# New hand-written engine orders behind the second score fill of a memory-augmented attention with a gated MLP

## The chip, the cores and the metric

The kernel runs on one core of a Trainium2 chip. A core has five engines that take their own instruction queues in order: PE (TensorE, matrix multiply), ACT (ScalarE), DVE (VectorE), POOL (GpSimd) and SP (SyncE, which here only issues DMAs). The metric is the device time of one execution in microseconds (us), the median of several runs.

## The reference

One sequence of 2048 tokens of width 512 goes through two branches, and a gate mixes them.

```python
q, k, v = x @ wq, x @ wk, x @ wv            # 32 heads of 16, 4 segments of 512 tokens
for s in range(4):
    p = softmax(qs @ ks.T * 0.25 + causal_mask)
    a_dot = p @ vs
    a_mem = (phi(qs) @ M) / (phi(qs) @ z + 1e-6)
    o = sigmoid(beta) * a_mem + (1 - sigmoid(beta)) * a_dot
    M = M + phi(ks).T @ vs;  z = z + phi(ks).sum()
a = concat(o) @ wo                          # phi(t) = t + 1 if t > 0 else exp(t)
b = (gelu(x @ w_gate) * (x @ w_up)) @ w_down    # inner width 1792
out = g * a + (1 - g) * b                   # g = sigmoid((x * gate_w).sum(-1))
```

All inputs and the output are bfloat16.

## The kernel before

The work is cut into some 1,200 named tasks, and `ORDER` is a table with one list of names for each engine: that is the order in which the engine executes. A name carries the segment first: `G0_12.2` is segment 0, tile 12 of the gate product, the piece that begins with its third matmul.

On PE, a *whole* task writes one PSUM bank of 128 x 512 and is cut into pieces of two matmuls (line 531): K, Q and V are the projections (four tiles each and segment), G and U the 14 tiles of the gate and up products, D the 4 token tiles of the down product with the wo product (18 matmuls: for segments 0 to 2 the four wo ones first, for segment 3 last). `qk0_1A1` is a *fill*: the scores of segment 0, head group 1, part A1, written as four row tiles into the four banks X (line 906). Parts A0, B0, A1, B1 are the two key halves of the even and the odd heads; part L, once in two head groups, is the diagonal's low corner. `numx1` is the memory's numerator and is filled in the same way (line 826). `pv0_1_0` is a P*V *burst* of 32 small matmuls in column tiles of 32 (lines 954 and 962), `mz0` a memory update (line 873), in column tiles as well. `num1` is a single matmul of the memory.

Whether a K, Q, V, G, U, D or num matmul runs whole or as four column tiles of 32 isn't written in the list: `column_runs` looks at each run of tasks between two fills, and if a burst or memory update stands in it, all matmuls of the run are issued as column tiles (line 533), so that PE keeps one mode in the run.

```python
for c in range(0, P, 32):
    r = e.matmul(view()[c:c + 32, :], lhsT[:, c:c + 32], rhs, start=first, stop=last,
                 tile_position=(0, c))
```

Beside the four X banks there are four banks W, which all whole tasks, bursts and updates share. A bank is free again when its contents are copied out: `K0_3ev`, `Vev0_1`, `Gev0_12` (lines 551 on ACT and 554 on DVE), `Um0_4` (gelu result times the up product, line 1053), `pvt0_0_1` (transposition of a burst's result, line 968), `mzacc0`, `fin`. Each such task stands in the list of ACT or of DVE.

After a fill, ACT makes `exp` of all four X banks (line 912), and the next fill may begin only then. POOL sets the causal corner of the result to zero (`msk`, line 915); a burst needs the masks of its parts and of L. DVE ends a head group with `norm` (lines 980 to 986), which needs both transposed bursts and `GdT`, the gates. The gates come from `gexp` (ACT, line 673), `gmat` (DVE, lines 676 to 679), `gbd` (POOL, lines 681 and 687: nine operations) and `omg` (POOL), and from the sums `gmul` and `gsum` over x times gate_w, `gexs` (ACT) and `exsT` (POOL, line 813). `mzbd0` on DVE (lines 887 and 892) multiplies the new memory by gbd; `numx1` and `num1` need it. `numd1`, `nump1` and `numl1` divide (lines 838 to 855) and free X and num1's bank. `pke`, `pkc`, `pqe`, `pqc` are the phi functions on ACT and DVE, `kp` (lines 763, 772) and `kl` (751) the padded keys.

SP issues the DMAs: `x2_0` to `x2_3` are transposing loads of segment 2's x (line 564; they wait for exp0_1B1), `w_wu`, `w_wd`, `w_wo` weights (each waits for an exp), `pkT` and `oTd` transpositions, `xt1` the untransposed x for gmul1 (it waits for mz0), `Vlo` copies of V rows for the low corner, `out` the results.

`schedule` walks the five lists with estimated durations. It doesn't change their order; its modelled times decide which of the four W banks a group takes, from the constants SWITCH (a change of mode), HOP (from one engine to another) and others.

Of the kernel before, what the change touches and what calls it, by code (L numbers as in the profile page):

```python
# [1203 lines left out]
```

## Time and profile before

| what | value |
|---|---|
| median of 3 runs | 264.63 us (264.21 to 264.8) |
| the profiled execution: time | 265.65 us |
| its span, first to last instruction | 264.4 us |
| granted TensorE clock, mean | 1.00 |
| PE matmuls at line 533 (column tiles) | 1348 instructions |

The profile's page gives busy times and shares, the chain of work that ended last, and groups of instructions; the timeline lists instructions in order of time (start us, length us, engine, line, operation, output<-inputs, shape, count, and in brackets the idle time before them with what ended it). A matmul's end in the timeline is modelled, so lengths overlap by some 0.16 us: the distance between two starts is what counts. PE is the matmul, PEld its weight load. "x10" counts instructions; one matmul in column tiles is four of them.

### The profile page before, as it was taken

What the parts mean: (1) busy time and instruction counts of PE and PEld (TensorE: products, weight loads), DVE (VectorE), ACT (ScalarE), POOL (GpSimd) and SP (SyncE); (2) the same over time, 40 slices, a digit from 0 to 9 for tenths busy, and PEclk for the clock granted to TensorE, in tenths of its full rate; (3) what the DMA queues carried; (4) which work ended last, traced back from release to release, by engine and by line L of the source; (5) the groups of instructions that cost most, each with busy time, mean ns of one, the idle gap of its engine ahead of it and who ended that gap; (6) DMA issues with size and microseconds to landing.
All of it is one profiled execution on the core that took longest, in us unless ns stands there. A gap on an engine that the chain in (4) does not pass through costs nothing.

```text
span 264.4 us, 9416 instructions
## 1 busy us (share of the span) xinstructions
PE 259.4 (98%) x4164; PEld 120.0 (45%) x4164; DVE 196.6 (74%) x369; ACT 212.2 (80%) x190; POOL 106.0 (40%) x256
## 2 busy tenths in 40 slices
PE   8799999999999999999999999999999999999996
PEld 4444445344544444544444444543455434454454
DVE  1589998898998978767795877679895765637363
ACT  3589999889999798799968888789986786877822
POOL 8216843815003464461460164256460233316520
PEclk9999999999999999999999999999999999999999
DMA  6973033940006956120003413310002031000102
GB/s 217 282 198 62 4 72 101 331 141 2 5 6 166 170 84 61 44 82 0 2 2 85 71 32 62 103 41 1 4 2 42 2 84 44 12 30 2 42 2 82
DMA packets 32776, 18.37 MB, mean 69 GB/s; under 512 B 20576, under 2 KB 32736, under 8 KB 32736
## 3 DMA queue, kind: packets, MB, share of 16 engines
q1 hardware_dynamic: 31632, 16.73, 27.5%
q10 hardware_dynamic: 1104, 1.05, 1.2%
q8 instruction: 32, 0.52, 0.8%
q14 instruction: 8, 0.07, 0.1%
HBM read 9.84 MB, written 2.10 MB: 45 GB/s over the span
## 4 chain that ended last, share of the span: by engine, by line
PE 91%; DMA 3%; DVE 2%; POOL 2%; ACT 1%; issue 1%; ACTq 0%; DVEq 0%
PE psW L531 47%; PE psW L533 25%; PE psXALL L906 9%; PE psW L954 5%; DMA wk<-in_A_wk_dram 3%; PE psXALL L533 1%; PE psW L962 1%; PE psXALL L531 1%; POOL gbd L681 1%; ACT pt L912 1%; PE psXALL L826 1%; DVE mzbd L892 1%; PE psW L873 0%; POOL pt L915 0%; DVE obf L984 0%
## 5 line engine op out<-in xcount | busy, mean ns | idle before, releaser
L912 ACT ACTIVATE pt<-psXALL 128x2048 bf16<-128x2048 f32 x64 | 120.1, 1876 | 23.2 <-PE psXALL L906 19.8
L915 POOL TENSOR_SCALAR_AFFINE_SELECT pt<-pt 128x256 bf16<-128x256 bf16 x128 | 57.3, 457 | 119.9 <-ACT pt L912 114.9
L1053 DVE TENSOR_TENSOR hT<-psW,hT 128x512 bf16<-128x512 f32 x56 | 37.6, 686 | 19.0 <-PE psW L531 15.0
L968 DVE STREAM_TRANSPOSE tb<-psW 128x512 f32<-128x512 f32 x32 | 22.3, 707 | 19.5 <-PE psW L962 19.3
L531 PE MATMUL psW<-wd,hT 128*128 128x512 bf16 x136 | 35.5, 380 | 0.0
L531 PE MATMUL psW<-xT,wu 128*128 128x512 bf16 x132 | 34.9, 380 | 0.0
L531 PE MATMUL psW<-xT,wg 128*128 128x512 bf16 x138 | 34.0, 379 | 0.0
L915 POOL TENSOR_SCALAR_AFFINE_SELECT ptl<-ptl 128x512 bf16<-128x512 bf16 x32 | 23.2, 726 | 10.9 <-ACT ptl L912 9.3
L906 PE MATMUL psXALL<-qT,kpad 32*128 32x320 bf16 (+3 forms) x512 | 25.4, 273 | 0.0
L533 PE MATMUL psW<-xT,wu 128*32 128x512 bf16 x368 | 22.0, 379 | 0.0
L533 PE MATMUL psW<-xT,wg 128*32 128x512 bf16 x344 | 20.9, 379 | 0.0
L1037 ACT ACTIVATE hT<-psW 128x512 bf16<-128x512 f32 x28 | 15.3, 598 | 6.6 <-PE psW L533 3.5
L813 POOL COPY exsT<-exs 32x4 f32<-32x4 f32 x64 | 14.1, 220 | 15.9 <-ACT exs L804 12.2
L531 PEld LDWEIGHTS psW<-xT,wg 128*128 128x128 bf16 x138 | 12.9, 98 | 16.0 <-DVE hT L554 0.5
L531 PEld LDWEIGHTS psW<-wd,hT 128*128 128x128 bf16 x136 | 12.5, 98 | 15.8 <-issue 2.1
L533 PE MATMUL psW<-wd,hT 128*32 128x512 bf16 x296 | 19.4, 380 | 0.0
L954 PE MATMUL psW<-pt,vaug 128*17 128x192 bf16 (+3 forms) x512 | 19.3, 273 | 0.0
L531 PE MATMUL psW<-xT,wk 128*128 128x512 bf16 (+1 forms) x74 | 17.2, 334 | 2.0 <-DMA wk<-in_A_wk_dram 1.5
L906 PEld LDWEIGHTS psXALL<-qT,kpad 32*128 32x128 bf16 x512 | 7.6, 92 | 24.7 <-ACT pt L912 14.0
L912 ACT ACTIVATE ptl<-psXALL 128x2048 bf16<-128x2048 f32 x8 | 15.0, 1878 | 4.6 <-PE psXALL L906 4.6
L531 PEld LDWEIGHTS psW<-xT,wu 128*128 128x128 bf16 x132 | 11.7, 98 | 14.7 <-issue 1.9
L531 PE MATMUL psW<-wv,xT 128*128 128x512 bf16 x58 | 16.5, 380 | 0.0
(122 smaller groups left out, 372.3 us busy)
## 6 DMA issues: line engine op xcount, KB each, us to landing
out_dram<-ost SPq DMA_DIRECT2D x15, 128.0 KB, 1.8
wg<-in_B_w_gate_dram SPq DMA_DIRECT2D x2, 896.0 KB, 7.9
wu<-in_B_w_up_dram SPq DMA_DIRECT2D x2, 896.0 KB, 7.0
wd<-in_B_w_down_dram SPq DMA_DIRECT2D x2, 896.0 KB, 5.7
phkt<-in_A_x_dram SPq DMA_DIRECT2D x3, 512.0 KB, 3.8
vlow<-vaug SPq DMA_DIRECT2D x8, 136.0 KB, 2.7
hT<-in_A_x_dram SPq DMA_DIRECT2D x2, 256.0 KB, 3.9
wq<-in_A_wq_dram SPq DMA_DIRECT2D x2, 256.0 KB, 6.1
```

The costliest lines, as they stand in the source:

```text
L531: return e.matmul(view(), lhsT, rhs, start=first, stop=last)
L533: r = e.matmul(view()[c:c + 32, :], lhsT[:, c:c + 32], rhs, start=first, stop=last, tile_position=(0, c))
L681: gb = task("gbd", POOL, [Instr(lambda e, c=c, j=j: e.tensor_tensor(gbd[32 * c:32 * c + 32, :, j, 0:16], gmat[32 * c:32 * c + 32, 2 * c + ...
L813: cross = task(f"exsT{s}", POOL, [Instr(lambda e, g=g, c=c: e.tensor_copy(exsT[sl][32 * g:32 * g + 32, c:16:4], exs[32 * c:32 * c + 32, s4 ...
L826: task(f"numx{s}", PE, [Instr(lambda e, g=g, i=i, qt=qt, t=t: e.matmul(X[g][:, 34 * i:34 * i + 34], phq[32 * g:32 * g + 32, t, qt * 128:(q ...
L906: instrs.append(Instr(lambda e, g=g, lhs=lhs, rhs=rhs, c0=c0, ncol=ncol: e.matmul(X[g][:, c0:c0 + ncol], lhs(32 * g), rhs(32 * g), start=T ...
L912: exp_task(s, f"exp{s}_{t}{name}", [Instr(lambda e: e.activation(dst[:], XALL[:, :].rearrange("p (g c) -> p g c", g=4), ACTF.Exp, scale=AT ...
L915: task(f"msk{s}_{t}{name}", POOL, [Instr(lambda e, view=view, pat=pat, base=base: e.affine_select(out=view, in_=view, compare_op=ALU.is_ge ...
L954: instrs.append(Instr(lambda e, t=t, q=q, kb=kb, slot=slot, c0=c0: e.matmul(gp.f32()[32 * q:32 * q + 17, 128 * kb + 64:512], Vaug[sl][:, k ...
L968: task(f"pvt{s}_{t}_{j}", DVE, [Instr(lambda e: e.transpose(Tb[:, j, :], gp.f32()[:, :]), [gp.key], [("Tb", j)], dve_t(512))], grp=gp)
L1037: lambda e, g=g, ft=ft, s=s: e.activation(hT[s % 2][:, ft, :], g.f32()[:, :], ACTF.Gelu_apprx_tanh),
L1053: task(f"Um{s}_{ft}", DVE, [Instr(lambda e, g=g, ft=ft: e.tensor_tensor(hT[sl][:, ft, :], g.f32()[:, :], hT[sl][:, ft, :], ALU.mult), [g.k ...
```

## The change

All five lists are made anew behind the second fill (`qk0_0B0`); up to there they are the same, apart from the places of DVE, ACT and POOL tasks that lie beside it. The same tasks are executed, with the same operations. 22 tasks of copying, summing and scaling go from ACT to DVE and 20 from DVE to ACT. Of the matmuls that can be tiled, 236 stand in a run with a burst or update in place of 337. In the planner, SWITCH and HOP get other values, and the change of mode is counted before a task's start instead of behind its end. The diff, cut to the first 65 us of PE and what goes with them, and PE's and SP's ends:

```diff
-SWITCH = 0.097
+SWITCH = 0.1
...
-        "V0_2.2 K0_2.4 K0_2.5 K0_2.6 K0_2.7 qk0_0A0 V0_0.0 G0_2.0 V0_0.2 G0_2.2 K0_3.4 V0_1.0 qk0_0B0 V0_3.0 "
-        "V0_3.2 K0_3.5 V0_1.2 K0_3.6 Q1_3.0 qk0_0L Q1_0.0 Q1_3.2 Q1_0.2 G0_1.0 K0_3.7 qk0_0A1 G0_1.2 Q1_1.0 "
-        "G0_12.0 Q1_1.2 G0_12.2 qk0_0B1 G1_10.0 G1_5.0 G1_5.2 G1_10.2 G1_9.0 qk0_1A0 pv0_0_0 G1_7.0 G1_7.2 G1_9.2 "
-        "G0_3.0 qk0_1B0 K1_0.0 G0_3.2 G0_6.0 K1_0.2 G0_6.2 qk0_1A1 pv0_0_1 G0_5.0 G0_5.2 G0_7.0 Q1_2.0 qk0_1B1 "
-        "Q1_2.2 G0_10.0 V1_1.0 V1_1.2 G0_7.2 qk0_2A0 G0_10.2 G1_11.0 G1_11.2 G1_2.0 G1_2.2 qk0_2B0 pv0_1_0 mz0 "
-        "pv0_1_1 G1_1.0 qk0_2L G1_8.0 G1_12.0 G1_12.2 G1_1.2 G1_8.2 qk0_2A1 V1_0.0 V1_0.2 K1_1.0 G1_6.0 G1_6.2 "
-        "qk0_2B1 K1_1.2 G0_9.0 G0_9.2 V1_3.0 K1_2.0 qk0_3A0 K1_2.2 V1_3.2 G1_0.0 G1_0.2 K1_3.0 K1_3.2 qk0_3B0 "
-        "pv0_2_0 G0_4.0 Q2_1.0 G0_4.2 Q2_1.2 G0_13.0 qk0_3A1 pv0_2_1 Q2_0.0 G0_13.2 Q2_0.2 G0_0.0 qk0_3B1 Q2_3.0 "
-        "G0_11.0 G0_0.2 G1_3.0 G1_3.2 Q2_3.2 G0_11.2 G0_8.0 num1 numx1 G1_4.0 G1_4.2 U0_4.0 G0_8.2 U0_4.2 U0_0.0 "
-        "U0_0.2 U0_1.0 U0_1.2 U0_3.0 U0_6.0 U0_3.2 G1_13.0 U0_9.0 U0_6.2 G1_13.2 U0_9.2 U0_5.0 U0_7.0 U0_5.2 "
-        "U0_11.0 U0_8.0 U0_7.2 U0_2.0 U0_2.2 U0_8.2 U1_5.0 U0_11.2 pv0_3_1 U1_5.2 qk1_0A0 pv0_3_0 U0_10.0 U0_10.2 "
-        "U1_0.0 U1_0.2 U1_8.0 U1_6.0 U1_6.2 U0_13.0 U0_13.2 qk1_0B0 U1_2.0 U1_12.0 U1_1.0 U1_12.2 U1_2.2 U1_8.2 "
...
-        "D3_1.8 D3_0.8 D3_2.12 D3_0.10 D3_1.10 D3_2.14 D3_1.12 pv3_3_1 D3_0.12 D3_3w0.0 D3_3w1.0 D3_3w0.4 D3_0.14 "
-        "D3_1.14 D3_3w0.8 D3_3w0.12 D3_1.16 D3_0.16 D3_2.16 D3_3a0.0 D3_3w1.4 D3_3w1.8 D3_3w1.12 D3_3a1.0 "
+        "V0_2.2 K0_2.4 K0_2.5 K0_2.6 K0_2.7 qk0_0A0 V0_0.0 G0_2.0 V0_0.2 G0_2.2 K0_3.4 V0_1.0 qk0_0B0 K0_3.5 "
+        "V0_1.2 V0_3.0 K0_3.6 K0_3.7 Q1_0.0 V0_3.2 qk0_0L Q1_0.2 G0_1.0 Q1_3.0 G0_1.2 Q1_3.2 qk0_0A1 G0_12.0 "
+        "G0_12.2 G0_3.0 G0_3.2 G1_10.0 qk0_0B1 G1_9.0 G1_7.0 G1_10.2 G1_9.2 G1_7.2 qk0_1A0 G1_5.0 Q1_2.0 G0_7.0 "
+        "G1_5.2 G0_7.2 pv0_0_0 qk0_1B0 K1_0.0 K1_0.2 V1_1.0 Q1_1.0 Q1_1.2 qk0_1A1 Q1_2.2 V1_1.2 G0_5.0 G1_12.0 "
+        "G0_5.2 qk0_1B1 pv0_0_1 G0_10.0 G1_12.2 G0_10.2 G1_2.0 G1_2.2 qk0_2A0 G1_1.0 G1_1.2 G0_6.0 G1_11.0 G0_6.2 "
+        "G1_11.2 qk0_2B0 mz0 pv0_1_0 V1_3.0 pv0_1_1 qk0_2L V1_3.2 G1_6.0 V1_0.0 V1_0.2 K1_3.0 qk0_2A1 K1_2.0 "
+        "K1_3.2 G1_6.2 K1_2.2 G1_0.0 qk0_2B1 Q2_1.0 G0_8.0 G1_8.0 G1_0.2 Q2_1.2 G0_8.2 qk0_3A0 G1_8.2 K1_1.0 "
+        "G0_4.0 K1_1.2 G0_4.2 pv0_2_1 qk0_3B0 G1_4.0 G1_4.2 G0_0.0 G0_0.2 pv0_2_0 qk0_3A1 Q2_0.0 G0_13.0 G0_9.0 "
+        "Q2_0.2 G0_9.2 qk0_3B1 num1 G0_13.2 G1_3.0 G1_3.2 Q2_3.0 Q2_3.2 numx1 G0_11.0 G0_11.2 U0_0.0 G1_13.0 "
+        "G1_13.2 U0_0.2 U0_1.0 U0_1.2 U0_2.0 U0_6.0 U0_2.2 U0_5.0 U0_5.2 U0_8.0 U0_3.0 U0_6.2 U0_3.2 U0_11.0 "
+        "U0_11.2 U0_8.2 U0_13.0 U0_13.2 U1_6.0 U1_6.2 U0_9.0 U1_0.0 U0_9.2 U1_0.2 U0_7.0 U0_7.2 U0_4.0 U1_5.0 "
+        "U1_5.2 qk1_0A0 U0_4.2 U1_9.0 U1_8.0 U1_8.2 U1_9.2 U1_1.0 U1_12.0 U1_12.2 U0_12.0 pv0_3_0 qk1_0B0 U1_1.2 "
+        "U1_7.0 U1_7.2 U0_12.2 pv0_3_1 qk1_0L U1_2.0 V1_2.0 V1_2.2 U1_3.0 U1_2.2 qk1_0A1 U1_3.2 D0_2.0 V2_3.0 "
...
+        "qk3_3B1 D3_2.6 D3_2.8 D3_0.10 pv3_3_0 D3_1.12 D3_3w0.0 D3_2.10 pv3_3_1 D3_2.12 D3_0.12 D3_3w0.4 D3_0.14 "
+        "D3_1.14 D3_3w0.8 D3_3w0.12 D3_2.14 D3_2.16 D3_1.16 D3_3w1.0 D3_0.16 D3_3a0.0 D3_3w1.4 D3_3w1.8 D3_3w1.12 "
+        "D3_3a1.0 "
...
-        "Vev0_2 exp0_0A0 Vev0_0 exp0_0B0 gsum0_1 exp0_0L K0_3ev exp0_0A1 gexs0 gexp exp0_0B1 pke0_1 exp0_1A0 "
-        "Gev1_7 exp0_1B0 K1_0ev exp0_1A1 pqe1_0 exp0_1B1 Q1_2ev exp0_2A0 Gev0_10 exp0_2B0 pqe1_1 exp0_2L Gev1_12 "
-        "exp0_2A1 Vev1_0 exp0_2B1 Gev0_9 exp0_3A0 K1_2ev Vev1_3 exp0_3B0 gsum1_0 gsum1_1 exp0_3A1 Q2_0ev gexs1 "
-        "exp0_3B1 Gev0_0 Gev1_3 gelu0_0 Gev1_4 Gev0_8 gelu0_2 gelu0_6 gelu0_10 gelu1_0 gelu1_7 exp1_0A0 kl1_00 "
...
+        "Vev0_2 exp0_0A0 gexp exp0_0B0 gsum0_1 exp0_0L Gev0_1 exp0_0A1 Gev0_12 exp0_0B1 pke0_1 exp0_1A0 Gev0_7 "
+        "gexs0 exp0_1B0 K1_0ev exp0_1A1 pqe1_0 exp0_1B1 Gev1_12 Gev0_10 exp0_2A0 Gev1_1 exp0_2B0 pqe1_1 exp0_2L "
+        "Vev1_0 exp0_2A1 K1_2ev exp0_2B1 gsum1_3 Q2_1ev exp0_3A0 K1_1ev Gev1_8 exp0_3B0 gexs1 Gev1_4 exp0_3A1 "
+        "Q2_0ev exp0_3B1 Gev0_13 gelu0_0 Gev0_11 Gev1_13 gelu0_2 gelu0_6 gelu0_10 gelu1_0 gelu1_7 exp1_0A0 kl1_00 "
...
-        "x0ev0a_0 x0ev0_1 x0ev1_1 kp0_1 kl0_10 kl0_11 kl0_01 Q0_3ev kp0_0 Q0_2ev pkc0_0 K0_2ev gmul0 Gev0_2 "
-        "gsum0_0 gsum0_3 Vev0_1 kl0_21 Vev0_3 gsum0_2 kl0_20 Q1_0ev kp0_2 kl0_30 Q1_3ev Gev0_1 Q1_1ev kp0_3 Gev1_5 "
-        "Gev0_12 Gev1_10 pvt0_0_0 kl0_31 gmat pkc0_1 Gev0_3 Gev1_9 Gev0_6 pvt0_0_1 GdT0 Gev0_5 norm0_0 Vev1_1 "
-        "Gev0_7 pqc1_0 Gev1_2 Gev1_11 pvt0_1_0 pvt0_1_1 pqc1_1 mzacc0 Gev1_8 Gev1_1 mzbd0 Gev1_6 gts0 norm0_1 "
-        "K1_1ev gmul1 kp1_00 Gev1_0 K1_3ev gsum1_2 pvt0_2_0 Gev0_4 Q2_1ev gsum1_3 pvt0_2_1 Gev0_13 gts1 norm0_2 "
-        "Q2_3ev Gev0_11 numd1 nump1_0 numl1 Um0_0 Um0_1 Um0_4 Um0_3 nump1_2 Um0_6 Um0_9 Gev1_13 Um0_5 nump1_3 "
-        "Um0_7 Um0_2 nump1_1 Um0_8 Um0_11 pvt0_3_1 Um1_5 pvt0_3_0 Um0_10 Um1_0 Um1_6 Um0_13 kl1_01 kp1_10 Um1_12 "
...
+        "x0ev0a_0 x0ev0_1 x0ev1_1 kp0_1 kl0_10 kl0_11 kl0_01 Q0_3ev kp0_0 Q0_2ev pkc0_0 K0_2ev gmul0 Gev0_2 Vev0_0 "
+        "gmat K0_3ev Vev0_3 Q1_0ev Vev0_1 gsum0_3 Q1_3ev kl0_21 kp0_2 kp0_3 Gev0_3 gsum0_0 Gev1_10 Gev1_9 kl0_30 "
+        "kl0_20 Gev1_7 kl0_31 gsum0_2 pvt0_0_0 Gev1_5 pkc0_1 Q1_1ev Q1_2ev Vev1_1 Gev0_5 pqc1_0 GdT0 pvt0_0_1 "
+        "Gev1_2 norm0_0 Gev0_6 Gev1_11 mzacc0 pvt0_1_0 mzbd0 pvt0_1_1 Vev1_3 norm0_1 K1_3ev Gev1_6 gmul1 gsum1_2 "
+        "Gev1_0 gsum1_1 Gev0_8 gsum1_0 Gev0_4 pvt0_2_1 pqc1_1 Gev0_0 gts1 pvt0_2_0 kp1_00 Gev0_9 norm0_2 Q2_3ev "
+        "Gev1_3 numd1 Um0_0 nump1_0 numl1 Um0_1 Um0_2 Um0_5 nump1_3 Um0_3 Um0_6 Um0_11 Um0_8 Um0_13 nump1_2 Um1_6 "
+        "Um1_0 nump1_1 Um0_9 Um1_5 Um0_4 Um0_7 Um1_8 Um1_9 kl1_01 Um1_12 kp1_01 Um1_1 pvt0_3_0 Um1_7 pvt0_3_1 "
...
-        "ident masks vones consts msk0_0A0 msk0_0B0 msk0_0L exsT0 msk0_0A1 msk0_0B1 omg msk0_1B0 msk0_1A0 msk0_1A1 "
-        "msk0_1B1 msk0_2B0 gbd msk0_2A0 msk0_2L msk0_2B1 msk0_2A1 msk0_3A1 msk0_3B0 msk0_3A0 msk0_3B1 msk1_0A0 "
...
+        "ident masks vones consts msk0_0A0 gbd msk0_0L msk0_0A1 msk0_0B1 msk0_0B0 omg exsT0 msk0_1A1 msk0_1A0 "
+        "msk0_1B1 msk0_1B0 msk0_2L msk0_2A0 msk0_2B0 msk0_2B1 msk0_2A1 exsT1 msk0_3B0 msk0_3B1 msk0_3A1 msk0_3A0 "
...
-        "x0_0 x0_1 w_wq0 w_wq1 w_wg0 x1_0 w_gwb x1_1 w_beta x1_2 x1_3 w_wg1 Vlo0_0 pkT0_0 Vlo0_1 pkT0_3 pkT0_2 "
-        "pkT0_1 x2_0 xt1 w_wu1 w_wu0 x2_1 x2_3 x2_2 w_wd1 oTd1_1 oTd1_0 w_wd0 oTd1_3 w_wo x3_1 Vlo1_1 x3_0 Vlo1_0 "
-        "oTd1_2 x3_2 x3_3 pkT1_2 pkT1_1 pkT1_0 pkT1_3 out0 xt2 oTd2_0 out1 out2 oTd2_1 oTd2_3 oTd2_2 Vlo2_1 Vlo2_0 "
...
-        "out8 out11 out10 out13 out12 out14 out15_0 out15_1 "
+        "x0_0 x0_1 w_wq0 w_wq1 w_wg0 x1_0 w_gwb x1_1 w_beta x1_2 x1_3 w_wg1 pkT0_0 Vlo0_0 Vlo0_1 pkT0_3 pkT0_2 "
+        "pkT0_1 x2_3 w_wu0 x2_1 x2_2 x2_0 xt1 w_wu1 oTd1_3 oTd1_1 w_wo w_wd0 oTd1_2 w_wd1 oTd1_0 Vlo1_1 Vlo1_0 "
+        "pkT1_1 x3_3 x3_0 pkT1_0 pkT1_3 pkT1_2 xt2 out2 x3_2 out0 x3_1 oTd2_1 Vlo2_0 out3 Vlo2_1 oTd2_2 oTd2_3 "
...
+        "out8 out9 out10 out11 out14 out13 out12 out15_0 out15_1 "
...
-HOP = {PE: 0.25, ACT: 0.07, DVE: 0.07, POOL: 0.10, SP: 0.0}
+HOP = {PE: 0.235, ACT: 0.07, DVE: 0.07, POOL: 0.10, SP: 0.0}
...
-                st = max(cur[e], ready_at[t.id])
+                st = max(cur[e] + (SWITCH if e == PE and t.tiled != mode else 0.0), ready_at[t.id])
...
-                if t.tiled != mode:
-                    t.finish += SWITCH
```

107 rows, old and new, of the table ORDER are left out of this document.

## The prediction

> **What bounds the kernel now.** I read the page's busy shares first, then the stretches between four fills, then the timeline of PE (TensorE) alone.
>
> ```profile
> span 264.4 us, 9416 instructions
> PE 259.4 (98%) x4164; PEld 120.0 (45%) x4164; DVE 196.6 (74%) x369; ACT 212.2 (80%) x190; POOL 106.0 (40%) x256
> ...
> PE 91%; DMA 3%; DVE 2%; POOL 2%; ACT 1%; issue 1%; ACTq 0%; DVEq 0%
> ```
>
> PE is busy 98% of the span and 91% of the chain that ended last is PE. A busy PE can still stream slowly, so I count what a run of matmuls between two score fills costs when nothing disturbs it.
>
> ```profile
> 38.67 2.33 PE L531 MATMUL psW<-xT,wg 128*128 128x512 bf16 x10
> 40.94 0.40 PE L906 MATMUL psXALL<-qT,kpad 32*128 32x320 bf16 x8
> ...
> 72.58 5.35 PE L533 MATMUL psW<-xT,wu 128*32 128x512 bf16 x96
> 77.76 0.61 PE L954 MATMUL psW<-pt,vaug 128*17 128x448 bf16 x16
> ...
> 84.06 2.76 PE L531 MATMUL psW<-xT,wu 128*128 128x512 bf16 x12
> 86.76 0.41 PE L906 MATMUL psXALL<-qT,klow 32*128 32x64 bf16 x32
> ```
>
> Start to start, ten whole matmuls take 40.94 - 38.67 = 2.27 us and twelve 86.76 - 84.06 = 2.70: 0.216 each, plus 0.11 once for the change of mode. In column tiles, 96 instructions are 24 matmuls of full width: 5.18 / 24 = 0.216 too. **A matmul costs the same whole or as four column tiles**; what costs is a change of mode. With these prices I go through every run of the timeline. From 65 us to the last matmul no run is longer than its count by more than 0.02 us, but five runs in the first 55 us are:
>
> ```profile
> 20.32 1.47 PE L531 MATMUL psW<-xT,wq 128*128 128x512 bf16 x6
> 22.37 0.40 PE L906 MATMUL psXALL<-qT,kpad 32*128 32x448 bf16 x8
> ```
> ```profile
> 25.29 2.50 PE L531 MATMUL psW<-xT,wg 128*128 128x512 bf16 x10
> 27.72 0.40 PE L906 MATMUL psXALL<-qT,kpad 32*128 32x448 bf16 x8
> ...
> 41.26 0.61 PE L954 MATMUL psW<-pt,vaug 128*17 128x448 bf16 x16
> 43.62 0.41 PE L906 MATMUL psXALL<-qT,klow 32*128 32x64 bf16 x32
> ...
> 49.15 0.61 PE L531 MATMUL psW<-xT,wk 128*128 128x512 bf16 x2
> 51.70 0.40 PE L906 MATMUL psXALL<-qT,kpad 32*128 32x448 bf16 x8
> 52.03 0.60 PE L531 MATMUL psW<-xT,wk 128*128 128x512 bf16 x2
> ...
> 54.33 1.04 PE L531 MATMUL psW<-xT,wk 128*128 128x512 bf16 x4 [0.40 <-DVE kT L554]
> 55.30 0.40 PE L906 MATMUL psXALL<-qT,kpad 32*128 32x320 bf16 x8
> ...
> 168.91 0.67 PE L873 MATMUL psW<-vaug,phkt 128*32 128x34 bf16 x64
> 170.97 0.40 PE L906 MATMUL psXALL<-qT,kpad 32*128 32x320 bf16 x8
> ```
>
> Eight and a half matmuls took 2.05 where 1.94 is due: 0.11 lost. Ten took 2.43 for 2.27: 0.16. The run with mz0, two P*V bursts and two matmuls took 2.36; the one at 168.91 (mz2, one burst, four matmuls) took 2.06, which less two matmuls (0.43) and with one burst more (0.56) makes 2.19: 0.17. Ten took 2.55 for 2.27: 0.28. Twelve took 3.27 for 2.70: 0.57. Together **1.29 us, all of the PE time behind the second fill that an order can win**; everything else on PE is the same work at the same price.
>
> Why PE waited in the dearest two is in the timelines of POOL (GpSimd) and DVE (VectorE):
>
> ```profile
> 44.26 3.49 POOL L681 TENSOR_TENSOR gbd<-gexp,bdmask 32x64 f32<-32x64 f32 x8
> ```
> ```profile
> 48.12 0.53 DVE L887 TENSOR_TENSOR mzc<-mzacc,gbd 128x136 bf16<-128x136 f32 x1 [0.50 <-POOL gbd L687]
> 48.68 1.70 DVE L892 COPY mzbd<-mzc 32x34 bf16<-32x34 bf16 x4
> ...
> 53.62 0.65 DVE L554 CAST kT<-psW 128x512 bf16<-128x512 f32 x1
> ```
>
> gbd stands in POOL's list behind a mask that is ready only at 43.4. DVE takes its queue in order, so mzbd0 waits for gbd, and behind it Gev1_6, norm0_1 and K1_1ev: K1_1's bank is copied out at 53.62, and PE, which has four banks to turn, stands until 54.33.
>
> **The change part by part.** *Column tiles.* Counted in the two lists, 965 matmuls can be tiled; 337 stand in runs with a P*V burst before, 236 after. Each run between two fills has one mode, so both lists have 75 fills, 76 runs and 150 changes of mode. PE loses 101 x 3 = 303 matmuls and as many weight loads (4164 to 3861). At 0.216 against 0.216 that is worth 0; the two pitches are equal to about 0.001, so between -0.1 and +0.1 us. Instruction fetch is worth 0: none of the five losses is PE's sequencer's.
>
> *gbd moves forward.* gexp goes behind the first exp, gmat to DVE's third place, gbd right behind msk0_0A0.
>
> ```profile
> 17.26 0.91 POOL L915 TENSOR_SCALAR_AFFINE_SELECT pt<-pt 128x256 bf16<-128x256 bf16 x2 [8.79 <-ACT pt L912]
> ...
> 22.38 2.84 POOL L915 TENSOR_SCALAR_AFFINE_SELECT ptl<-ptl 128x512 bf16<-128x512 bf16 x4 [1.53 <-ACT ptl L912]
> ```
> ```profile
> 17.12 0.69 DVE L554 CAST hT<-psW 128x512 bf16<-128x512 f32 x1 [0.34 <-PE psW L531]
> ...
> 29.72 0.41 DVE L676 TENSOR_SCALAR gtmp<-gexp 128x32 f32<-128x32 f32 x1
> ...
> 30.90 0.41 DVE L732 TENSOR_SCALAR kT<-kT 128x1024 bf16<-128x1024 bf16 x1
> ```
>
> Gev0_2 (the row at 17.12) keeps its place; a copy lasts 0.69 and the next starts some 0.6 after it. Vev0_0 comes second, gmat third, 30.90 - 29.72 = 1.18 long: from 18.3 to 19.5. gbd takes 3.49 + 0.2, to 23.4; msk0_0L 2.84, to 26.2; msk0_0A1 0.9, to 27.1; msk0_0B1 waits for its exp (fill at 25.25 on the undisturbed PE, 0.46 to the start, 1.88) and ends at 28.5; msk0_0B0 at 29.4. pv0_0_0, which needs it, stands at 30.3 in the new list, two microseconds later than before. **0.9 us are left; the stall goes.** mzbd0 then finds gbd ready for 20 us. What is late next is DVE itself, below.
>
> *The rest of the lists.* I placed every PE piece at the time that it has if PE never waits (0.216 a matmul, 0.11 a change, 0.33 a fill), from the second fill on, and added the queues of ACT, DVE and POOL against it with durations of these rows. ACT (ScalarE):
>
> ```profile
> 38.80 1.88 ACT L912 ACTIVATE pt<-psXALL 128x2048 bf16<-128x2048 f32 x1 [0.23 <-PE psXALL L906]
> 40.57 0.59 ACT L551 ACTIVATE hT<-psW 128x512 bf16<-128x512 f32 x1
> ```
>
> A fill comes every 2.6 us; exp and one copy take 1.77 + 0.59. Where the new list has a 1.05 us phi exp or two copies in one period, the next fill comes close: qk0_2A1 (needed 47.46) has 0.05 us left. On DVE the new list puts nine copies and two gate sums in and takes nine copies, one sum and gts0 out before numd1, about 0.3 us more. In my sum mzbd0 (at its mean in the other rows, below) ends at 46.0, K1_3ev at 50.0 with Q2_1 taking its bank at 50.4 (0.24 left), and numd1 starts 0.7 after PE could let it; Um0_0 frees U0_6's bank with 0.03 left, Gev0_11 that of U0_1 with 0.06. Nowhere do I find less than nothing, up to the last matmul; the last four pieces and the copies and stores behind them are the same. For the handful of places under 0.1 us I add 0.25 in all, since the sums are good to 0.1 each; the bounds are 0 and the 1.3 of before.
>
> *Queues that steps are moved past.* SP (SyncE) now issues w_wu0 between x2_3 and the other x2, xt1 behind all x2, w_wu1 behind xt1, and w_wo and both w_wd behind oTd1_3 and oTd1_1. The last are issued near 82 to 85 us for uses from 90 to 97: covered. x2 and xt1 are the second rival. SWITCH, HOP and the start rule steer only which bank a group takes.
>
> **Sum.** -1.29 + 0.25 + 0 = -1.04 us. The profiled execution took 265.65 around its span of 264.4; that becomes 264.6 with a span of 263.4. The median shown is 264.63, 1.0 under the profiled one; with the same difference I predict **263.6 us**. 0.2% (0.53 us) is about what can be told from no change here.
>
> **The rivals.**
>
> *DVE becomes the bound (0.19).*
>
> ```profile
> 17.56:65.11 47.55, 47.01 (x713) 20.20 (x713) 44.02 (x86) 43.59 (x44) 26.48 (x69) 1.00 0.42 106
> ```
> ```profile
> L892 DVE COPY mzbd<-mzc 32x34 bf16<-32x34 bf16 x12 | 3.3, 277 | 0.4
> ```
>
> In this stretch DVE (third sum) is busy 44.0 of 47.55 us, and the new one is to be 46.3 long with 44.3 of work. Four mzbd copies at the mean of 277 ns are 1.1; before they took 1.70, with POOL working. If such stretching costs DVE another microsecond, the copies come later, the banks too, and the stall is only moved: 264.6, the same. Against it: POOL is idle from 40 to 47 in the new list while mzbd0 runs.
>
> *The weights stand ahead of the x2 transposes (0.08, slower).*
>
> ```profile
> 43.11 1.85 SPq L568 DMA_DIRECT2D wu<-in_B_w_up_dram x2
> 45.00 5.21 SPq L564 DMA_TRANSPOSE xT<-in_A_x_dram x3
> ```
> ```profile
> xT<-in_A_x_dram SPq DMA_TRANSPOSE x4, 6.8
> ```
>
> x2_3 goes out at 38.7 (end of exp0_1B1). With three transposes at 1.74 (5.21 / 3) and w_wu0 at 0.93 ahead, x2_0 is issued at 44.8. At 6.8 us to landing it arrives at 51.6, and Q2_1.0 wants it at 50.4, six microseconds earlier than before. PE, in order, would stand 1.2; xt1, 1.74 behind, would hold gmul1 and all copies behind it on DVE. At 2 us of waiting the time is 265.6; from a landing after 52.0 (50.4 + 1.04 + 0.53) the kernel is slower than before. Against it: the 6.8 were measured behind two halves of wu, now one is ahead; I expect 48 to 49.
>
> *gbd meets DVE's fast copies (0.05).*
>
> ```profile
> 22.50 1.42 DVE L763 TENSOR_SCALAR kpad<-kT,maskc 128x512 bf16<-128x512 bf16 x2
> ...
> 26.35 0.63 DVE L763 TENSOR_SCALAR kpad<-kT,maskc 128x512 bf16<-128x512 bf16 x2
> ```
>
> The same pair took 1.42 us beside msk0_0L and 0.63 beside the small exsT copies. If gbd, now at 19.6 to 23.4, and the masks behind it stretch likewise by 2 us, msk0_0B0 ends at 31.4 and PE stands 1.1 at pv0_0_0: 264.7. Between 19.6 and 23.4 DVE has copies from PSUM, a sum and kl0_21 in the new list; both kpad pairs come behind, beside msk0_0L as before. The Trainium skill ("SBUF — State Buffer", Who interferes with whom) says that a DVE operation in a two-port mode and a GpSimd one exclude each other for a whole instruction; the stretched pair agrees, and read strictly it would give this rival's time.
>
> **How the numbers follow.** Forecast 0.66 (263.0 to 264.1), DVE 0.19 (264.2 to 265.0), transfer 0.08 (265.2 to 266), gbd 0.05 (264.3 to 265.0), something unseen and slower 0.02. Below 264.1: 0.70 with the mild ends of the rivals; within 0.2%: 0.19; above 265.2: 0.11. The low end is all of 1.29 won (263.3) less the 0.4 by which the lowest run lies under the median; the high end is 265.0: **262.9 to 265.0**.
>
> **What would show it.** PE: 3861 matmuls, 944 of them at the column-tile line; runs of ten at 2.27 us between 20 and 55 us; numx1 near 64.1 instead of 65.1; no wait of mzc for gbd. I am wrong if DVE's copies come later against their matmuls around U0_1 to U0_6 (64 to 70 us), if a DMA ends a wait of PE near 50 us, or if column tiles show a pitch other than 0.216.

## The result, and the profile after

The changed kernel takes 263.5 us (median of 16 runs, 262.53 to 264.39), the kernel before 264.42 beside it (16 runs, 263.96 to 264.8): a ratio of 0.9967, interval 0.9955 to 0.9978. A later comparison gave 263.39 (12 runs) against 264.36 (23 runs), 0.9968 [0.9952, 0.9984]. One run below, with all matmuls in column tiles, scatters by 3% in itself; its ratio counts the executions near its fastest alone (two of the six).

Both kernels were profiled twice, so that what an order does can be told from what the start and the end of an execution do:

| stretch (us) | before | after | before, second | after, second |
|---|---|---|---|---|
| start of the second fill, qk0_0B0 | 17.56 | 16.06 | 16.58 | 16.17 |
| from there to the last matmul's end | 244.83 | 243.62 | 244.81 | 243.60 |
| from there to the span's end | 2.04 | 2.08 | 2.04 | 2.49 |
| span | 264.4 | 261.8 | 263.4 | 262.3 |

The first two profiles differ by 2.6 us of span, but 1.50 of that lies ahead of the second fill, where PE's list is the same. In the timeline of PE the kernel before has this row at the start, and the changed one has no wait there:

```profile
8.70 1.14 PE L531 MATMUL psW<-xT,wk 128*128 128x256 bf16 x9 [1.47 <-DMA wk<-in_A_wk_dram]
```

The third part of wk landed at 8.56 us there and at 7.04 in the profile of after; in the second profile of before it landed at 6.85, and the wait was gone. The same kernel has it both ways, so it doesn't come from the order. What the orders did is the second row of the table: **1.21 us, twice, to 0.01.** The page of the changed kernel:

```profile
span 261.8 us, 8784 instructions
PE 258.5 (99%) x3861; PEld 119.9 (46%) x3861; DVE 195.5 (75%) x371; ACT 212.2 (81%) x185; POOL 105.0 (40%) x256
...
PE 97%; DMA 1%; DVE 0%; issue 0%
```

PE's share of the chain went from 91 to 97%; DVE, POOL and ACT, which held 5% of it, have all but left it. The timeline of PE shows the runs that were too long before:

```profile
16.06 0.40 PE L905 MATMUL psXALL<-qT,kpad 32*128 32x320 bf16 x8
...
21.49 2.33 PE L530 MATMUL psW<-xT,wg 128*128 128x512 bf16 x10
23.75 0.40 PE L905 MATMUL psXALL<-qT,kpad 32*128 32x320 bf16 x8
...
41.19 0.67 PE L872 MATMUL psW<-vaug,phkt 128*32 128x34 bf16 x64
...
43.41 0.41 PE L905 MATMUL psXALL<-qT,klow 32*128 32x64 bf16 x32
...
46.35 1.04 PE L530 MATMUL psW<-xT,wk 128*128 128x512 bf16 x4
...
48.62 0.40 PE L905 MATMUL psXALL<-qT,kpad 32*128 32x320 bf16 x8
48.94 0.60 PE L530 MATMUL psW<-xT,wq 128*128 128x512 bf16 x2
...
51.64 0.40 PE L905 MATMUL psXALL<-qT,kpad 32*128 32x448 bf16 x8
```

Ten matmuls take 2.26 us (from 21.49) and 2.27 (from 46.35), twelve take 2.70 (from 48.94), and the run with mz0, two bursts and two matmuls 2.22. Against their counts the runs behind the second fill are 0.16 us too long in all; before it was 1.34 (the prediction's 1.29 and 0.05 at mz1). POOL and DVE show why (timelines of the changed kernel; these times are 1.5 us earlier than on the scale of the prediction):

```profile
17.70 2.88 POOL L680 TENSOR_TENSOR gbd<-gexp,bdmask 32x64 f32<-32x64 f32 x8 [1.03 <-DVE gexp L678]
20.65 0.20 POOL L686 CAST gbd<-bdmask 128x8 f32<-128x8 bf16 x1
21.00 2.84 POOL L914 TENSOR_SCALAR_AFFINE_SELECT ptl<-ptl 128x512 bf16<-128x512 bf16 x4
...
26.15 1.75 POOL L914 TENSOR_SCALAR_AFFINE_SELECT pt<-pt 128x256 bf16<-128x256 bf16 x4 [1.42 <-ACT pt L911]
```
```profile
43.20 0.26 DVE L886 TENSOR_TENSOR mzc<-mzacc,gbd 128x136 bf16<-128x136 f32 x1
43.49 0.80 DVE L891 COPY mzbd<-mzc 32x34 bf16<-32x34 bf16 x4
...
47.93 0.65 DVE L553 CAST kT<-psW 128x512 bf16<-128x512 f32 x1
```

gbd runs at 17.7 and is done at 20.85; mzc starts at 43.20 without a wait, and the copy of K1_3 ends at 48.58, 0.36 us ahead of Q2_1.0, which takes its bank.

### The profile page after: what moved, and what is told of

Its sections match the earlier page's. It is cut to its first block, busy times and chain, and to the rows that moved or that the text cites. A ratio compares the mean times of both kernels' runs of the same rounds, so it can differ in the third digit from the quotient of the medians.

```text
span 261.8 us, 8784 instructions
## 1 busy us (share of the span) xinstructions
PE 258.5 (99%) x3861; PEld 119.9 (46%) x3861; DVE 195.5 (75%) x371; ACT 212.2 (81%) x185; POOL 105.0 (40%) x256
## 2 busy tenths in 40 slices
DMA packets 32774, 18.33 MB, mean 70 GB/s; under 512 B 20576, under 2 KB 32736, under 8 KB 32736
## 3 DMA queue, kind: packets, MB, share of 16 engines
q1 hardware_dynamic: 31632, 16.73, 30.3%
## 4 chain that ended last, share of the span: by engine, by line
PE 97%; DMA 1%; DVE 0%; issue 0%
PE psW L530 59%; PE psW L532 17%; PE psXALL L905 9%; PE psW L953 6%; PE psXALL L532 2%; PE psW L961 1%; DMA hT<-in_A_x_dram 1%; PE psXALL L530 1%; PE psW L872 1%; PE psXALL L825 1%; PE psXALL L632 1%; DVE obf L1084 0%
## 5 line engine op out<-in xcount | busy, mean ns | idle before, releaser
L1052 DVE TENSOR_TENSOR hT<-psW,hT 128x512 bf16<-128x512 f32 x56 | 36.7, 681 | 15.7 <-PE psW L530 11.4
L530 PE MATMUL psW<-xT,wg 128*128 128x512 bf16 x192 | 45.7, 379 | 0.0
L530 PE MATMUL psW<-xT,wu 128*128 128x512 bf16 x166 | 41.8, 380 | 0.0
L914 POOL TENSOR_SCALAR_AFFINE_SELECT ptl<-ptl 128x512 bf16<-128x512 bf16 x32 | 23.0, 718 | 44.2 <-ACT ptl L911 42.4
L967 DVE STREAM_TRANSPOSE tb<-psW 128x512 f32<-128x512 f32 x32 | 22.6, 710 | 17.8 <-PE psW L961 17.7
L530 PE MATMUL psW<-wd,hT 128*128 128x512 bf16 x134 | 34.9, 380 | 0.0
L530 PEld LDWEIGHTS psW<-xT,wg 128*128 128x128 bf16 x192 | 18.1, 98 | 21.5 <-issue 0.4
L530 PEld LDWEIGHTS psW<-xT,wu 128*128 128x128 bf16 x166 | 15.1, 98 | 19.1 <-issue 1.9
L532 PE MATMUL psW<-wd,hT 128*32 128x512 bf16 x304 | 20.1, 380 | 0.0
L953 PE MATMUL psW<-pt,vaug 128*17 128x192 bf16 (+3 forms) x512 | 19.5, 273 | 0.0
L953 PEld LDWEIGHTS psW<-pt,vaug 128*17 128x17 bf16 x512 | 12.2, 91 | 10.0 <-issue 1.2
L530 PE MATMUL psW<-xT,wk 128*128 128x512 bf16 (+1 forms) x70 | 15.5, 333 | 0.0
L532 PE MATMUL psW<-xT,wu 128*32 128x512 bf16 x232 | 14.3, 380 | 0.0
```

Source lines behind the costliest of these rows:

```text
L530: return e.matmul(view(), lhsT, rhs, start=first, stop=last)
L914: task(f"msk{s}_{t}{name}", POOL, [Instr(lambda e, view=view, pat=pat, base=base: e.affine_select(out=view, in_=view, compare_op=ALU.is_ge ...
L953: instrs.append(Instr(lambda e, t=t, q=q, kb=kb, slot=slot, c0=c0: e.matmul(gp.f32()[32 * q:32 * q + 17, 128 * kb + 64:512], Vaug[sl][:, k ...
L967: task(f"pvt{s}_{t}_{j}", DVE, [Instr(lambda e: e.transpose(Tb[:, j, :], gp.f32()[:, :]), [gp.key], [("Tb", j)], dve_t(512))], grp=gp)
L1052: task(f"Um{s}_{ft}", DVE, [Instr(lambda e, g=g, ft=ft: e.tensor_tensor(hT[sl][:, ft, :], g.f32()[:, :], hT[sl][:, ft, :], ALU.mult), [g.k ...
```

## The experiments

All times beside an experiment are medians, with the ratio to the kernel before in the same comparison. "Behind the second fill" is the stretch of the second row above: 244.83 before, 243.62 after.

### Three tasks forward in the old lists

The kernel before, with gexp, gmat and gbd moved forward and nothing else changed; 337 matmuls stay in column tiles.

```diff
-ACT:  exp0_0A0 Vev0_0 exp0_0B0 ... exp0_0A1 gexs0 gexp exp0_0B1
+ACT:  exp0_0A0 gexp Vev0_0 exp0_0B0 ... exp0_0A1 gexs0 exp0_0B1
-DVE:  Gev0_2 gsum0_0 gsum0_3 ... kl0_31 gmat pkc0_1
+DVE:  Gev0_2 gsum0_0 gmat gsum0_3 ... kl0_31 pkc0_1
-POOL: msk0_0A0 msk0_0B0 ... msk0_2B0 gbd msk0_2A0
+POOL: msk0_0A0 gbd msk0_0B0 ... msk0_2B0 msk0_2A0
```

> Before with three tasks moved: gexp behind the first exp, gmat behind gsum0_0, gbd behind msk0_0A0. If gbd's place is the cause of the two dearest waits, these 0.28 and 0.57 us go, and perhaps the 0.17 at mz0 stays: 0.6 to 0.9 us under before. If the banks turn too slowly for DVE's whole order and gbd is only where it shows, the waits move to the next copies: within 0.3 us of before.

Measured: 263.53 us (12 runs, 263.0 to 264.52), 0.9956 [0.994, 0.9973]; behind the second fill 243.80. Its timelines of PE, of DVE and of POOL:

```profile
47.39 0.61 PE L527 MATMUL psW<-xT,wk 128*128 128x512 bf16 x2
...
49.66 0.40 PE L902 MATMUL psXALL<-qT,kpad 32*128 32x448 bf16 x8
49.98 0.60 PE L527 MATMUL psW<-xT,wk 128*128 128x512 bf16 x2
...
52.68 0.40 PE L902 MATMUL psXALL<-qT,kpad 32*128 32x320 bf16 x8
```
```profile
46.10 1.47 DVE L888 COPY mzbd<-mzc 32x34 bf16<-32x34 bf16 x4
```
```profile
44.35 2.98 POOL L911 TENSOR_SCALAR_AFFINE_SELECT ptl<-ptl 128x512 bf16<-128x512 bf16 x4 [0.72 <-ACT ptl L908]
```

These are the two dearest runs of before, in the old order: 2.27 and 2.70 us now, where they took 2.55 and 3.27. The earlier 0.16 is gone too, so that the gain of the median, 1.0 us, is a little over the 0.6 to 0.9 expected; of the smaller waits some 0.2 in all are left. **Three moved tasks bring 1.03 of the 1.21 us, and the whole gain of the median**, without a single matmul fewer in column tiles.

### gbd late in the new lists

```diff
-POOL: msk0_0A0 gbd msk0_0L ... msk0_1B0 msk0_2L msk0_2A0 msk0_2B0 msk0_2B1
+POOL: msk0_0A0 msk0_0L ... msk0_1B0 msk0_2B0 gbd msk0_2L msk0_2A0 msk0_2B1
```

> The changed kernel with one thing undone: on POOL gbd stands late again, behind msk0_2B0, which stands behind msk0_1B0 as it did before; gexp and gmat stay early. Theory (gbd's place was the cause): msk0_2B0 can end at 44.2 us (its exp ends at 43.26), gbd 3.2 to 3.5 us later, at 47.4 to 47.7, and mzbd0 starts then in place of 43.20. norm0_1 and the copy K1_3ev behind it on DVE come 4.2 to 4.5 us late; K1_3ev had 0.35 us to spare before Q2_1.0, so PE waits about 4 us near 49 us: 266.5 to 267.7, with a wait of mzc for gbd in the records. Rival (the other places in the new lists made the gain, gbd's place is hidden): within 0.5 us of 263.5.

Measured: 268.62 us (4 runs, 268.3 to 269.68), 1.016 [1.0133, 1.0187]; behind the second fill 249.09, 5.47 more than the changed kernel. Timelines of DVE and PE, and busy time by stretch (PE, PEld, DVE, ACT, POOL, then the granted clock, DMA share, GB/s):

```profile
47.37 0.30 DVE L881 TENSOR_TENSOR mzc<-mzacc,gbd 128x136 bf16<-128x136 f32 x1 [4.16 <-POOL gbd L681]
```
```profile
46.45 0.61 PE L525 MATMUL psW<-xT,wk 128*128 128x512 bf16 x2 [0.86 <-ACT vaug L545]
46.99 0.40 PE L900 MATMUL psXALL<-qT,kpad 32*128 32x448 bf16 x8
49.96 1.89 PE L525 MATMUL psW<-xT,wk 128*128 128x512 bf16 x4 [2.58 <-DVE tb L962]
51.65 1.06 PE L525 MATMUL psW<-xT,wg 128*128 128x512 bf16 x2
```
```profile
47.39:49.96 2.57, 0.00 (x0) 0.00 (x0) 2.42 (x7) 1.88 (x1) 2.35 (x4) 1.00 1.05 369
49.96:53.39 3.43, 3.43 (x9) 1.20 (x10) 3.30 (x7) 0.00 (x0) 1.24 (x3) 0.50 0.00 0
```

DVE waits 4.16 us for gbd, as the theory has it, and the rival falls. PE's waits are 0.86 + 2.58 = 3.44, somewhat less than the 4 expected, and elsewhere. The long one is for the bank of a burst, emptied by the transposition behind mzbd0, which is late before K1_3's is. The short one is for a bank that ACT copies out; what ties it to gbd isn't shown. Most of the rest is not a wait: for 3.4 us behind the hole the granted clock is 0.50 (four matmuls from 49.96 to 51.65, 1.69 us in place of 0.86), which costs 1.7 us and takes the time above the 267.7 expected at most.

### The new lists in halves

One kernel has the new lists as far as numx1 and the old ones behind it (335 matmuls tiled), the other the old ones as far as numx1 and the new ones behind (232 tiled). At the seam, each drops what has been done; in the first, G0_11 has come to stand ahead of numx1.

```diff
 PE of the first:  ... Q2_3.2 G0_11.0 G0_11.2 numx1
-U0_0.0 G1_13.0 G1_13.2 U0_0.2 U0_1.0 ...
+U0_4.0 U0_4.2 U0_0.0 U0_0.2 U0_1.0 ...
 PE of the second: ... num1 G0_8.2 G1_4.0 G1_4.2 numx1
-U0_4.0 U0_4.2 U0_0.0 U0_0.2 U0_1.0 ...
+U0_0.0 G1_13.0 G1_13.2 U0_0.2 U0_1.0 ...
```

> The new lists up to numx1 (by the planner's own order of all five engines), the old lists for every task behind it. 335 matmuls stand in column tiles, nearly as many as the 337 of before. If the whole gain is the waits of PE in the first 55 us, this kernel has it: numx1 near 1.2 us earlier after the second fill, and a time 0.9 us (0.6 to 1.2) under before. If the gain comes from the fewer column tiles or from the new lists further on, it is gone: within 0.3 us of before.

> The reverse: the old lists up to numx1, the new ones behind it, 232 matmuls in column tiles. If the gain is the waits of the first 55 us: the five waits stand as before and the time is within 0.3 us of before. If it is the fewer column tiles or the later lists: 0.6 to 1.2 us under before.

Measured: 264.38 us (12 runs), 0.9993 [0.9978, 1.0008], for the new head; 265.42 (12 runs), 1.0039 [1.0021, 1.0058], for the new tail. Neither median says what it seems to. In the first, PE runs from the second fill to 62.5 us without a wait, as in the changed kernel, but around the seam it loses 1.46 us, 0.31 of it just ahead of numx1 and 0.99 behind (timeline of PE):

```profile
62.83 1.04 PE L525 MATMUL psW<-xT,wg 128*128 128x512 bf16 x4 [0.15 <-ACT hT L545]
63.80 0.62 PE L820 MATMUL psXALL<-mzc,phq 32*128 32x34 bf16 x60
64.39 2.77 PE L527 MATMUL psW<-xT,wu 128*32 128x512 bf16 x48
67.97 1.64 PE L527 MATMUL psW<-xT,wu 128*32 128x512 bf16 x24 [0.80 <-DVE phkt L849]
```

The larger of the two is for num1's bank: the old tail needs it where, behind the new head, it is still full. So this kernel can't show the gain in its time; that the waits ahead of 62.5 us are gone is what it shows. In the second, the two dearest of the old waits stand, the first grown from 0.28 to 0.52 us:

```profile
49.83 0.60 PE L525 MATMUL psW<-xT,wk 128*128 128x512 bf16 x2 [0.36 <-DVE hT L548]
...
53.00 1.04 PE L525 MATMUL psW<-xT,wk 128*128 128x512 bf16 x4 [0.40 <-DVE kT L548]
```

The two near 20 and 24 us stand as well, the one at mz0 is gone, and 0.15 at 31.86 is new. With 105 matmuls fewer in column tiles the waits of PE in this kernel are 1.71 us; less these, the stretch behind the second fill is 243.65 us, against 243.49 before (244.83 less 1.34): **the tiles bring nothing.** The second is slower than before by 0.5 us behind the second fill and 0.65 in the last stores, on which more below.

### No column tiles, and all column tiles

```diff
-            if any(u.tiled == "pv" for u in run):
+            if False:
```
```diff
-            if any(u.tiled == "pv" for u in run):
+            if not any(u.name.startswith("warm") for u in run):
```

> The changed kernel with no projection or MLP matmul in column tiles: the 236 matmuls of the runs with a burst or memory update are issued whole, and PE changes its mode around each burst, 190 times behind the first fill in place of 150, with 708 matmul instructions fewer. Theory (a change of mode costs 0.11 us and a matmul the same whole or tiled): 40 x 0.11 = 4.4 us more, 267.9, with the extra time only in runs that hold a burst. Rival (column tiles carry a cost that the pitch doesn't show, in weight loads or instruction supply): the loss is under 3 us or turns into a gain.

> After, with every run behind the first fill issued as column tiles: 917 matmuls in place of 236, 2043 more matmul and as many more weight-load instructions, the same 150 changes of mode. If a column-tiled matmul costs what a whole one costs (0.216 us either way): within 0.3 us of after. If the 101 tiles less brought the gain of 0.92 us, 681 more cost 6.2 us.

Measured without tiles: 271.4 us (4 runs, 270.78 to 272.0), 1.0258 [1.0232, 1.0284], worse than either theory. Run by run against the changed kernel, a run with one burst in its midst is 0.20 longer, with the burst at its edge 0.10, with two apart 0.42: 40 more changes of mode cost 4.1 us, **0.103 each**, as in the theory. Most of the other 4.7 us is one hole and what follows it (timeline of PE, then busy time by stretch):

```profile
43.59 0.23 PE L961 MATMUL psW<-ptl,vlow 128*17 128x64 bf16 x8
46.19 0.29 PE L961 MATMUL psW<-ptl,vlow 128*17 128x64 bf16 x8 [2.36 <-issue]
```
```profile
43.80:46.19 2.39, 0.03 (x6) 0.01 (x2) 0.56 (x4) 0.56 (x1) 0.00 (x0) 0.95 1.54 117
46.19:49.40 3.21, 3.21 (x46) 1.45 (x47) 2.03 (x4) 1.88 (x1) 0.33 (x1) 0.50 1.08 354
```

PE stops within a burst; all other engines are soon idle, the DMAs full. "issue" means that the profile shows nothing that PE waited for. What was missing, by the next experiment, were instructions: PE's instruction queue moves 16 KB packets, and one of them ran late, from 43.35 to 44.68 us; PE went on 1.5 behind it.

All in column tiles: 273.55 us (6 runs, 267.43 to 274.96), 1.0167 [1.0104, 1.023], with 5904 matmuls. The profiled execution is the longest of the six. Its waits of PE (in total, times, longest):

```profile
PE psW L532 <- issue: 4.5, 4, 1.8
PE psXALL L905 <- issue: 2.7, 1, 2.7
```

The 7.2 us of these five holes and a clock of 0.50 from 91.04 to 97.87, of which PE worked 6.0 and so lost 3.0, make 10.2 of the 11.5 us that this execution has more behind the second fill. Between the holes the pitch is 0.216. Neither expectation holds: the tiles cost no pitch, but the time is 4 to 11 us over the changed kernel. So a tiled matmul costs what a whole one costs as long as its four instructions arrive.

### Instruction supply or not

The kernel without tiles again, with one DMA moved.

```diff
-SP: pkT0_1 x2_3 w_wu0 x2_1 x2_2 x2_0 xt1 w_wu1
+SP: pkT0_1 x2_3 x2_1 x2_2 x2_0 xt1 w_wu0 w_wu1
```

> The kernel with no projection or MLP matmul in column tiles, which took 271.4 us, with one more edit: on SP w_wu0 moves behind xt1, so that no half of wu is on the DMAs before 44 us. There PE stood 2.36 us at 43.8 us with nothing that released it but instruction supply (a 16 KB packet of the instruction queue ran only from 43.3 to 44.6, in the midst of the wu and x2 transfers), and its granted clock was 0.50 for 3.4 us behind it. Theory (the packet was late because the weights stood ahead of it on the DMAs): the packet runs by 42, the hole and the slow stretch go, worth 2.4 + 1.4 us: 267.5 to 268.2, which is the 40 changes of mode at 0.10 alone. Rival (the packet is asked for late, or the x2 transposes hold it as well): the hole stays within 0.5 us, 271; or it moves to the next packet at 50 us with the weights now there.

Measured: 268.38 us (4 runs, 267.43 to 269.67), 1.0158 [1.0133, 1.0183]; 3.0 us won by moving one DMA that PE does not need for another 20 us, and 0.2 above the range of the theory. The packet now runs from 41.9 to 42.8, and the hole shrinks (timeline of PE):

```profile
44.19 0.24 PE L956 MATMUL psW<-ptl,vlow 128*17 128x64 bf16 x8 [0.37 <-issue]
```

The clock stays at 1.00. Behind the second fill it is 5.24 us over the changed kernel: 4.1 of changes of mode, and the rest mostly this hole and another of 0.4. The theory holds in the main; the rival keeps a small part, since the packet still comes 0.4 late, with the x2 transposes ahead of it.

### The transfers in the changed kernel

w_wu1 moved ahead, and in another kernel w_wu0 moved behind.

```diff
-SP: pkT0_1 x2_3 w_wu0 x2_1 x2_2 x2_0 xt1 w_wu1
+SP: pkT0_1 x2_3 w_wu0 w_wu1 x2_1 x2_2 x2_0 xt1
```
```diff
-SP: pkT0_1 x2_3 w_wu0 x2_1 x2_2 x2_0 xt1 w_wu1
+SP: pkT0_1 x2_3 x2_1 x2_2 x2_0 xt1 w_wu0 w_wu1
```

> The changed kernel with w_wu1 moved on SP from behind xt1 to right behind w_wu0, so that both halves of wu go out ahead of x2_1, x2_2, x2_0 and xt1. In the changed kernel x2_0 lands at 47.0 us and Q2_1.0 needs it at 48.9; xt1 lands at 48.5 and gmul1 starts at 49.1. Theory (the transfer's slack of 1.9 us is real and small): a half of wu takes 5 us from issue to landing there, so x2_0 lands near 51 to 52 and xt1 near 53; PE waits 2 to 3 us at Q2_1.0 with a DMA as releaser, and DVE some 4 us at gmul1, whose followers hold PE by another 0 to 1.5 us: 265.5 to 268. Rival (transfers share the queues and the order on SP decides little): within 0.5 us of 263.5.

> The changed kernel with w_wu0 moved on SP behind xt1, so that both halves of wu come last. Theory (no wait of PE hangs on wu, whose first use is at 64 us): within 0.2 us of the changed kernel, 263.5. Rival (the instruction packet of 50 us now meets the weights, or the first U matmul meets a late wu1): a hole of 0.5 to 2 us, 264 to 265.5.

Measured with wu ahead: 264.9 us (10 runs, 263.94 to 266.35), 1.0017 [0.9995, 1.0039]; behind the second fill 245.44, 1.82 more. The timelines of PE and of DVE show one hole that was not expected and part of what was:

```profile
49.90 0.60 PE L525 MATMUL psW<-xT,wg 128*128 128x512 bf16 x2 [1.20 <-issue]
...
51.63 0.60 PE L525 MATMUL psW<-xT,wq 128*128 128x512 bf16 x2
...
55.52 0.62 PE L527 MATMUL psW<-xT,wk 128*32 128x512 bf16 x8 [0.25 <-ACT qT L545]
```
```profile
53.01 1.22 DVE L787 TENSOR_TENSOR phkt<-phkt,gwb 128x2048 bf16<-128x2048 bf16 x1 [1.77 <-DMA phkt<-in_A_x_dram]
```

The hole is a late instruction packet: it ran from 47.4 to 48.4 here (44.35 to 45.42 in the changed kernel, whose start was 1.3 us earlier). x2_0 landed at 51.46 and Q2_1.0 started at 51.63: without the hole PE would have been there at 50.43 and waited about 1.0 for it. The run can't part the two, since each hides the other. What was expected of xt1 came, but smaller: it landed at 52.98, DVE waited 1.77 us for it with gmul1, ACT's gsum1_3 and Q2_1ev came behind that, and PE had to wait for a bank that Q2_1ev empties. Against the pitch PE lost 1.36 us at the hole and 0.42 there, together nearly all of the 1.82. With wu behind: 263.41 (12 runs, 262.88 to 264.13), 0.9965 [0.9951, 0.9979], and 243.61 behind the second fill: the theory holds, and the slack is real on that side.

### The planner's constants

```diff
-SWITCH = 0.1
+SWITCH = 0.097
-HOP = {PE: 0.235, ACT: 0.07, DVE: 0.07, POOL: 0.10, SP: 0.0}
+HOP = {PE: 0.25, ACT: 0.07, DVE: 0.07, POOL: 0.10, SP: 0.0}
-                st = max(cur[e] + (SWITCH if e == PE and t.tiled != mode else 0.0), ready_at[t.id])
+                st = max(cur[e], ready_at[t.id])
...
+                if t.tiled != mode:
+                    t.finish += SWITCH
```

> The new five lists with the planner of before: SWITCH 0.097, HOP 0.25 for PE, the change of mode counted behind a task's end. Theory (these steer only which of four banks a group takes, and any choice that the model finds free is nearly as good): within 0.3 us of 263.5, waits of PE behind the second fill under 0.4 us. Rival (the new constants were needed for the new lists): single waits of 0.2 us or more at a bank, 264 or above.

Measured: 263.51 us (10 runs, 263.03 to 265.47), 0.9967 [0.9947, 0.9986]; 243.61 behind the second fill, waits 0.15. The new constants are worth nothing that can be told.

### Both kernels once more

No edit.

> The changed kernel once more, for a second profile and a tighter ratio. Theory: the order alone is worth 1.2 us, and the median 0.9 to 1.2 less than before; the start (landing of the third wk load, 7.0 or 8.5 us) shifts single runs by 1.5 us whatever the order. Rival: the 1.2 us of the profiled pair was luck, and the gain is 0.6 or less.

> The kernel before once more, for a second profile: the same five waits behind the second fill, 1.2 to 1.4 us in all, at the same places whether or not the third wk load lands late. Rival: the waits move with the start and are chance.

Measured: 263.39 us against 264.36, as above, and for the kernel before one execution of 264.69. Its five waits are 0.10, 0.16, 0.18, 0.25 and 0.58 us, 0.10, 0.16, 0.16, 0.28 and 0.57 in the first profile: the same places and sizes, though PE started 0.98 us earlier. They belong to the order. In the second profile of the kernel before, the waits of PE list the last one:

```profile
PE psW L531 <- DVE kT L554: 0.4, 1, 0.4
```

## Why the prediction was right, point by point

- **The 1.29 us that an order can win.** Right: 1.21 won, 0.16 of waits left (0.08 of them at mz1, where 0.05 stood before).
- **The cause, gbd behind a late mask.** Right, and shown from both sides: forward in the old lists, with gexp and gmat, it wins 1.03 us of PE; back in the new ones it loses 5.47, of which 3.4 are waits and 1.7 the lower clock behind them. The sums of the queues held. With 1.5 us for the earlier start, gmat ran at 18.33 to 19.12 (predicted 18.3 to 19.5), gbd ended at 22.35 (23.4; it took 3.15 us, not 3.69), msk0_0B0 at 29.40 (29.4) with pv0_0_0 at 30.34 (30.3), mzbd0 at 45.79 (46.0), K1_3ev at 50.08 (50.0), Q2_1.0 at 50.44 (50.4), numx1 at 64.27 (64.1).
- **Column tiles at 0.** Right for PE (3861 matmuls, 944 of them at the column-tile line, as counted): the kernel with only the three tasks moved is as fast with 337 as the changed one with 236. Its reason was thin. "Instruction fetch is worth 0" rested on no loss being PE's sequencer's; the wait that fetch makes carries another name, "issue", and three experiments ran into it. By the changed kernel's packet (landed at 45.42) and the 1.47 us that PE needed behind a packet with wu ahead, PE could go past 47.22 from 46.9 on: 0.3 us to spare, an estimate. The step held because the new lists happened to leave it that; the prediction hadn't worked it out, so this part is luck. The Trainium skill ("Runtime: NRT & Kernel Launch", Instruction fetch mechanics) says that crossing a 16 KiB boundary is "mostly hidden"; the changed kernel agrees in all its 30 packets, the kernel without tiles does not, with 2.36 us at one.
- **0.25 for new small waits.** Too much: 1.29 less the 1.21 won is 0.08, so that 0.17 of it was not needed.
- **Stores behind the last matmul "the same".** Wrong, by 0.2 us. From the last matmul to the end it is 1.98 to 2.69 us, 2.27 in the mean of the seven profiles that have the changed kernel's end of PE's list and its column tiles; four with the old end have 2.04 each, and the two without column tiles, which have the new end, 1.94 each. The last issues of SP, in the two profiles of the changed kernel and in the first of before:

```profile
258.01 1.60 SPq L567 DMA_DIRECT2D out_dram<-ost  x3
```
```profile
258.11 2.01 SPq L567 DMA_DIRECT2D out_dram<-ost  x3
```
```profile
260.94 1.34 SPq L568 DMA_DIRECT2D out_dram<-ost  x3
```

  The second of these three issues takes 0.55 and 0.96 us in the changed kernel and 0.33 before. PE's last instruction packet goes with it: it ran from 257.80 to 258.76 and from 257.97 to 259.27 there, and the issue ended 0.38 and 0.37 us behind it; in all eight profiles where the two meet, the one with all matmuls tiled among them, that distance is 0.33 to 0.38. With the old end the packet stops 2.27 us or more ahead of the issue's end, and without column tiles 0.23 and 0.24 ahead of its start; in these six profiles it takes 0.33. With 303 matmuls fewer, the last packet falls on the last stores. So the smaller number of tiles, costed at 0, seems to cost 0.2 by where the instruction stream's packets fall. 1.21 less 0.2 comes near the 0.92 and 0.97 by which the medians differ; that nothing else stands between is argued, not shown. The 0.17 too much for small waits and these 0.2, which the prediction put at nothing, nearly cancel: that the forecast of 263.6 came within 0.1 us of the median is partly luck.
- **From the profiled execution to the median.** Right: its 1.0 us over the median was the late wk at the start.
- **DVE as the bound, and gbd beside DVE's fast copies.** Neither rival came. Busy time of DVE in the stretch from the second fill to numx1 (third sum):

```profile
16.06:62.77 46.71, 46.71 (x729) 21.18 (x729) 42.44 (x83) 43.27 (x41) 27.43 (x80) 1.00 0.48 93
```

  DVE has 42.4 us of work in 46.7, where the sum had 44.3 in 46.3, and PE is busy all of it. The reason that spoke against the first rival was the right one: POOL is idle while mzbd0 runs. Four mzbd copies took 0.80 us then, 1.70 before, and 1.47 in the experiment with the three tasks, beside the masks in the rows shown there. The Trainium skill ("SBUF — State Buffer", Who interferes with whom) says that a DVE operation in a two-port mode and a GpSimd one exclude each other for a whole instruction; the copies agree in kind. gbd itself, beside DVE's copies from PSUM, took 3.15 us, no longer than before.
- **Weights ahead of x2.** It did not come: x2_0 landed at 47.0 us, 1.9 ahead of Q2_1.0 (48.5 on the prediction's scale, where 48 to 49 was expected). With the other half of wu ahead as well, the time is 1.4 us more, but in another shape: a late instruction packet and a late xt1, with any wait for x2_0 hidden behind the first.
